# LN2's variance and bias on ScalarE, squares from the raw sum, and a new order of all queues: an adaLN block with sliding-window attention and a gated FFN

## Chip, cores and metric

One NeuronCore of one Trainium2 chip runs the whole program. The metric is the device time of one execution in microseconds; the time before is the median of three runs. All times on the trace count from the start of the profiled span.

## What is computed

```python
mod = (silu(c) @ w_mod).reshape(1, 6, 1, -1)        # sa, ca, ga, sb, cb, gb
h = layernorm(x) * (1 + ca) + sa
x = x + ga * A(h, wqkv, wo)      # 32 heads of 16; each position looks at 8 earlier ones, 2 apart
h = layernorm(x) * (1 + cb) + sb
x = x + gb * ((silu(h @ w1) * (h @ w3)) @ w2)
```

x has 2048 positions of 512 columns, the FFN is 1792 wide, all bf16. A layernorm takes mean and variance over the 512 columns. The first is called LN1 here, the second LN2.

## The kernel before

The 2048 positions are 16 tiles T of 128. Each stage is a set of ops that Python code records, and each op has one engine and a key. In the texts an op is called by its key, as here:

- LN1 (ln_stats, lines 549 to 580): statistics on VectorE and GpSimd, normalization on VectorE. Then q, k and v products on TensorE (lines 691, 711), evacuated by ScalarE (700, 701, 721). v goes to DRAM.
- Attention per tile: `pq` (line 742) is VectorE's product of q with eight shifted copies of k, 128x4096. `lg` on TensorE (752) sums it by head into logits. `sm` are five VectorE ops of the softmax (764, 769, 794 to 797) around `ex`, the exponential on ScalarE (782); it works on two tiles at a time. `at` turns the weights on TensorE (807), evacuated by ScalarE (811). `vl` are four loads of shifted v by SP. `av` is VectorE's product of v and weights (827), 128x4096. `ac` on TensorE (855) sums it, evacuated by ScalarE (861). `ot` is a transposing DMA. `wo` is the output product (867). `rs` is VectorE's residual sum (871), which also gives the row's sum `sx`.
- LN2 (ln_sums, lines 582 to 604), by pairs of tiles (0,1), (2,3) and so on: `nm = -sx/512` on GpSimd (586); squares of `x + nm` with their sum on ScalarE (590), for each tile; variance plus epsilon (596), the power -0.5 (597) and the bias `nm * rs` (599) on GpSimd; normalization `x*rs + nb` on ScalarE (601), for each tile. ln_T then transposes, by TensorE (636, evacuated at 644) for the groups 0 and 1, by DMA (`tr`) for the groups 2 to 5, which ScalarE then scales and shifts in place (621).
- FFN in six groups of tiles: (0,1), (2,3), (4..7), (8..11), (12,13), (14,15). `Fg.f` is column block f (of 14) of group g. It has two halves on TensorE (883), four matmuls each, of 256 columns where the group has two tiles and 512 where it has four: the gate, which ScalarE takes through Silu (889), and the up half, which VectorE multiplies with it (892). `zT.0` and `zT.1` are the two halves of tile T's output product (921; 909 for the last two tiles, which are cut by columns), each over seven blocks. `zo` adds x on VectorE (931), and SP stores. `mod7` to `mod10` scale w2's rows by gb on VectorE (952).

Silu and the exponential need different tables on ScalarE; a load of 1.28 us stands at each of the nine switches. `lg` and `ac` use a quarter of TensorE's columns at a time (tiled products).

Every result has a buffer from a pool: eight PSUM banks, 20 buffers of FFN products, five of normalized rows, three of shifted v, and so on. An op that writes a buffer waits for all users of the value that held it before. All engines take their instructions in order.

The order isn't found by a scheduler at run time. `ORDER` lists all ops by number, `SLOTS` a buffer for every pooled value, and `Program.place` cuts `ORDER` into one queue for each engine and for SP. `Program.synchronize` puts in the waits that the recorded dependences need, including waits of an engine for an own earlier result. Each op carries a planned `cost` in ns for whoever works such a list out, and a `lock` flag that marks the long VectorE products and GpSimd's ops. ScalarE's small new ops have a planned cost of 80, the power 600.

Of the kernel before, what the change touches and what calls it, by code (L numbers as in the profile page):

```python
# [10 lines left out]
P = 128  # L11
# [245 lines left out]
def c_act(n):  # L257
    return 66 + n * 107 // 128
# [14 lines left out]
def _build(p, A_x, A_wqkv, A_wo, B_w1, B_w3, B_w2, c, w_mod, out):  # L273
# [308 lines left out]
    def ln_sums(Ts):  # L582

        n, i, k = len(Ts), Ts[0], ("st", NT + Ts[-1])
        vnm, vvs, vns = Val("nmean"), [], [Val("xn", xnpool) for T in Ts]
        p.op("pool", lambda e: e.tensor_scalar(nm[:, i:i + n, 0], sx[:, i:i + n, 0], -1.0 / D, None, op0=ALU.mult), 215, k,  # L586
             r=[vsx[T] for T in Ts], w=[vnm])
        for T, vn in zip(Ts, vns):
            vv = Val("var")
            p.op("act", lambda e, vn=vn, T=T: e.activation(vn.at[:], x_sb[:, T, :], ACT.Square, bias=nm[:, T, :],  # L590
                                                    accum_out=var[:, T, :]), c_act(512) + 212, ("st", NT + T), r=[vx[T], vnm],
                 w=[vv, vn])
            vvs.append(vv)
        va, vr, vb = Val("vare"), Val("rstd"), Val("nbias")
        rsn = rs[:, NT + i:NT + i + n, 0]
        o = p.op("pool", lambda e: e.tensor_scalar(rsn, var[:, i:i + n, 0], 1.0 / D, EPS, op0=ALU.mult, op1=ALU.add), 210, k, r=vvs, w=[va])
        o = p.op("pool", lambda e: e.tensor_tensor(rsn, rsn, bass.AP(cst, 1, [[2, P], [0, n]]), ALU.pow), 600, k, r=[va, vcst],
                 w=[vr], lead=o)
        p.op("pool", lambda e: e.tensor_tensor(nb[:, i:i + n, 0], nm[:, i:i + n, 0], rsn, ALU.mult), 210, k, r=[vr, vnm], w=[vb], lead=o)  # L599
        for T, vn in zip(Ts, vns):  # L600
            p.op("act", lambda e, vn=vn, T=T: e.activation(vn.at[:], x_sb[:, T, :], ACT.Identity, bias=nb[:, T, :],  # L601
                                                           scale=rs[:, NT + T, :]),
                 c_act(512) + 212, ("nm", NT + T), r=[vx[T], vr, vb], w=[vn])
        return vns
# [472 lines left out]
```

## Time and profile before

| what | value |
|---|---|
| median of 3 runs | 238.1 us (237.95 to 238.78) |
| profiled execution, own time | 239.43 us |
| its span on the trace | 237.7 us |
| granted TensorE clock | 1.00 throughout |
| squares, line 590 | 16 of 0.71 us, and 16 reads of the accumulator of 0.19 |
| variance 596, power 597, bias 599 on GpSimd | 8 each, median 0.19, 0.70 and 0.20 us |
| normalization, line 601 | 16 of 0.81 us |
| products of VectorE, lines 742 and 827 | 16 each, 2.28 and 2.29 us |

A line of the profile's groups gives the source line, engine, operation, output and inputs by the program's names, shapes and count, then busy time and the mean ns of one, then the idle time ahead of it and what ended it. A line of the waits gives engine and line, what it waited for, and microseconds in all, times and the longest. A line of the timeline gives start and length in microseconds. A busy TensorE is one that has a matmul under way; matmuls overlap, so a wait shorter than one's fill shows only in the distance of their starts: 0.109 us for 256 columns and 0.216 for 512 when nothing is in the way.

### The profile page before, as it was taken

The page shows a single profiled execution, that of the slowest core. Times are in us where ns is not written, and L with a number is a line of the kernel's source. Part 1 is how long each engine was busy: PE and PEld are TensorE (multiplying, and loading weights), DVE is VectorE, ACT ScalarE, POOL GpSimd, SP SyncE. Part 2 cuts the span into 40 slices and gives each one's busy share as a digit, 9 for nine tenths or more (in the row PEclk, how much of TensorE's full clock was granted, in tenths as well). Part 3 has the DMA queues.
Part 4 walks back from the last instruction along what each step waited for, and adds up shares of the span by engine and source line. Part 5 has one row for each costly group of instructions (what it writes and reads, how often), then busy time and mean ns, then how long its engine had stood idle before and what let it go on. Part 6 is the DMA issues. An engine that isn't in the chain of part 4 may idle for free.

```text
span 237.7 us, 4535 instructions
## 1 busy us (share of the span) xinstructions
PE 229.7 (97%) x1781; PEld 136.2 (57%) x1806; DVE 179.4 (75%) x279; ACT 138.5 (58%) x267; POOL 29.2 (12%) x66
## 2 busy tenths in 40 slices
PE   7999999999999998999999999999999999999995
PEld 4776454445588674664444444444475457485774
DVE  5699999999999989999999999682654403434433
ACT  2289577999978744985865594837473405040300
POOL 4434100013002000240002520012010000000000
PEclk9999999999999999999999999999999999999999
DMA  6999999999999999897981693642203000000202
GB/s 216 372 337 322 158 237 299 208 269 283 353 200 270 243 249 199 173 260 177 247 234 47 182 234 72 154 132 46 67 19 91 3 0 0 6 19 0 70 0 88
DMA packets 46317, 38.85 MB, mean 163 GB/s; under 512 B 21704, under 2 KB 37080, under 8 KB 46296
## 3 DMA queue, kind: packets, MB, share of 16 engines
q1 hardware_dynamic: 46288, 38.56, 66.9%
q8 instruction: 14, 0.23, 0.4%
q14 instruction: 7, 0.06, 0.1%
q10 hardware_dynamic: 8, 0.00, 0.0%
HBM read 29.62 MB, written 4.21 MB: 142 GB/s over the span
## 4 chain that ended last, share of the span: by engine, by line
PE 74%; DMA 8%; DVE 8%; SPq 4%; ACT 3%; issue 2%; ACTq 0%; DVEq 0%
PE pall L883 38%; PE pall L921 18%; DMA sb_x<-in_A_x_dram 5%; PE pall L867 5%; SPq L124 4%; PE pall L691 4%; DMA sb_vsh<-v_scratch_dram 3%; PE pall L909 3%; PE pall L855 2%; PE pall L752 2%; PE pall L711 2%; DVE sb_vsh L827 2%; DVE sb_pq L742 2%; DVE sb_hh L892 1%; ACT sb_h L621 1%
## 5 line engine op out<-in xcount | busy, mean ns | idle before, releaser
L883 PE MATMUL pall<-sb_h,sb_w 128*128 128x256 bf16 (+1 forms) x664 | 101.9, 307 | 1.8 <-DVE sb_hh L892 0.9
L883 PEld LDWEIGHTS pall<-sb_h,sb_w 128*128 128x128 bf16 x672 | 64.8, 98 | 37.2 <-issue 2.8
L889 ACT ACTIVATE sb_sg<-pall 128x256 bf16<-128x256 f32 (+1 forms) x84 | 35.6, 453 | 54.1 <-PE pall L883 53.0
L892 DVE TENSOR_TENSOR sb_hh<-sb_sg,pall 128x256 bf16<-128x256 bf16 (+1 forms) x84 | 39.9, 505 | 34.8 <-PE pall L883 32.7
L921 PE MATMUL pall<-sb_w,sb_hh 128*128 128x512 bf16 x190 | 44.0, 379 | 0.3
L742 DVE TENSOR_TENSOR sb_pq<-sb_q,sb_kT 128x4096 bf16<-128x4096 bf16 x16 | 36.3, 2282 | 0.0
L921 PEld LDWEIGHTS pall<-sb_w,sb_hh 128*128 128x128 bf16 x196 | 19.0, 98 | 21.6 <-DVE sb_hh L892 0.4
L691 PE MATMUL pall<-sb_h,sb_wqkv 128*128 128x512 bf16 (+1 forms) x154 | 30.2, 335 | 0.5 <-issue 0.2
L827 DVE TENSOR_TENSOR sb_vsh<-sb_vsh,sb_al 128x4096 bf16<-128x4096 bf16 x12 | 27.3, 2287 | 2.1 <-DMA sb_vsh<-v_scratch_dram 2.1
L621 ACT ACTIVATE sb_h<-sb_h,sb_modc 128x512 bf16<-128x512 bf16 (+1 forms) x24 | 16.5, 743 | 10.1 <-DMA sb_h<-sb_xn 10.1
L691 PEld LDWEIGHTS pall<-sb_h,sb_wqkv 128*128 128x128 bf16 x160 | 14.7, 98 | 11.8 <-ACT sb_ac L861 0.4
L931 DVE TENSOR_TENSOR sb_o<-pall,sb_x 128x512 bf16<-128x512 f32 (+1 forms) x18 | 11.1, 625 | 10.5 <-PE pall L921 6.8
L711 PE MATMUL pall<-sb_wqkv,sb_h 128*128 128x512 bf16 x62 | 15.5, 379 | 0.2
L867 PE MATMUL pall<-sb_wo,sb_ot 128*128 128x512 bf16 x61 | 15.3, 379 | 0.3 <-issue 0.2
L586 POOL TENSOR_SCALAR sb_nm<-sb_sx 128x2 f32<-128x2 f32 x8 | 1.7, 218 | 105.2 <-DVE sb_x L871 105.1
L644 ACT ACTIVATE sb_h<-pall,sb_modc 128x256 bf16<-128x256 bf16 (+1 forms) x18 | 9.9, 612 | 7.5 <-DVE sb_modc L509 6.5
L861 ACT ACTIVATE sb_ac<-pall 128x512 bf16<-128x512 f32 x16 | 9.5, 595 | 7.2 <-PE pall L855 7.1
L601 ACT ACTIVATE sb_xn<-sb_x,sb_nb,sb_rs 128x512 bf16<-128x512 bf16 x16 | 12.4, 806 | 0.7 <-POOL sb_nb L599 0.6
L871 DVE SCALAR_TENSOR_TENSOR sb_x<-pall,sb_x 128x512 bf16<-128x512 f32 x16 | 10.9, 686 | 1.5 <-PE pall L867 1.3
L590 ACT ACTIVATE sb_xn<-sb_x,sb_nm 128x512 bf16<-128x512 bf16 x16 | 11.4, 714 | 0.7 <-POOL sb_nm L586 0.7
L721 ACT ACTIVATE sb_v<-pall 128x512 bf16<-128x512 f32 x16 | 9.5, 600 | 2.8 <-PE pall L711 2.8
L555 DVE BATCH_NORM_STATS2 sb_st<-sb_x 128x6 f32<-128x512 bf16 x16 | 10.6, 680 | 0.8 <-DMA sb_x<-in_A_x_dram 0.7
(87 smaller groups left out, 208.3 us busy)
## 6 DMA issues: line engine op xcount, KB each, us to landing
sb_vsh<-v_scratch_dram SPq DMA_DIRECT2D x48, 256.0 KB, 5.5
sb_vshx<-v_scratch_dram SPq DMA_DIRECT2D x16, 256.0 KB, 4.6
sb_w<-in_B_w_dram SPq DMA_DIRECT2D x6, 512.0 KB, 7.9
sb_w<-in_B_w_dram SPq DMA_DIRECT2D x6, 384.0 KB, 5.4
v_scratch_dram<-sb_v SPq DMA_DIRECT2D x16, 128.0 KB, 6.4
out_dram<-sb_o SPq DMA_DIRECT2D x14, 128.0 KB, 1.8
sb_wqkv<-in_A_wqkv_dram SPq DMA_DIRECT2D x6, 256.0 KB, 6.3
sb_x<-in_A_x_dram SPq DMA_DIRECT2D x4, 256.0 KB, 6.4
```

What stands on the lines that cost most here:

```text
L590: p.op("act", lambda e, vn=vn, T=T: e.activation(vn.at[:], x_sb[:, T, :], ACT.Square, bias=nm[:, T, :], accum_out=var[:, T, :]), c_act(512 ...
L601: p.op("act", lambda e, vn=vn, T=T: e.activation(vn.at[:], x_sb[:, T, :], ACT.Identity, bias=nb[:, T, :], scale=rs[:, NT + T, :]), c_act(5 ...
L621: return e.activation(vh.at[:, ft, 0:n * P], vh.at[:, ft, 0:n * P], ACT.Identity, bias=modc[:, 8 * which + ft:8 * which + ft + 1], scale=m ...
L691: ins = e.matmul(bank(vp)[:, j * n:(j + 1) * n], wqkv[:, t, col:col + P], vh.at[:, t, 0:n], start=(t == ORDER[0] and j == 0), stop=(t == O ...
L711: ins = e.matmul(bank(vp), vh.at[:, t, tt * P:(tt + 1) * P], wqkv[:, t, 2 * D:3 * D], start=(t == ORDER[0]), stop=(t == ORDER[-1]))
L742: return e.tensor_tensor(vp.at[:], in0, in1, ALU.mult)
L827: return e.tensor_tensor(v_w, v_w, a_w, ALU.mult)
L867: ins = e.matmul(bank(vy), vt.at[:, ft, :], wo[:, ft, :], start=(ft == 0), stop=(ft == KT - 1))
L883: ins = e.matmul(bank(vp)[:, 0:n], wt[:, t, fi * P:(fi + 1) * P], vh.at[:, t, 0:n], start=(t == 0), stop=(t == KT - 1))
L889: p.op("act", lambda e: e.activation(vt.at[:, 0:n], bank(vgp)[:, 0:n], ACT.Silu), c_act(n), k, r=[vgp], w=[vt], table="silu")
L892: p.op("dve", lambda e: e.tensor_tensor(vh_.at[:, 0:n], vt.at[:, 0:n], bank(vup)[:, 0:n], ALU.mult), c_dve(n), k, r=[vt, vup], w=[vh_])
L921: ins = e.matmul(bank(vz), vhh[fi].at[:, tt * P:(tt + 1) * P], w2[:, fi, :], start=(fi == 0), stop=(fi == NF - 1))
```

## The change

```diff
-            p.op("act", lambda e, vn=vn, T=T: e.activation(vn.at[:], x_sb[:, T, :], ACT.Square, bias=nm[:, T, :],
-                                                    accum_out=var[:, T, :]), c_act(512) + 212, ("st", NT + T), r=[vx[T], vnm],
+            p.op("act", lambda e, vn=vn, T=T: e.activation(vn.at[:], x_sb[:, T, :], ACT.Square, bias=sx[:, T, :], scale=-float(D),
+                                                    accum_out=var[:, T, :]), c_act(512) + 212, ("st", NT + T), r=[vx[T], vsx[T]],
...
-        o = p.op("pool", lambda e: e.tensor_scalar(rsn, var[:, i:i + n, 0], 1.0 / D, EPS, op0=ALU.mult, op1=ALU.add), 210, k, r=vvs, w=[va])
-        o = p.op("pool", lambda e: e.tensor_tensor(rsn, rsn, bass.AP(cst, 1, [[2, P], [0, n]]), ALU.pow), 600, k, r=[va, vcst],
-                 w=[vr], lead=o)
-        p.op("pool", lambda e: e.tensor_tensor(nb[:, i:i + n, 0], nm[:, i:i + n, 0], rsn, ALU.mult), 210, k, r=[vr, vnm], w=[vb], lead=o)
+        p.op("act", lambda e: e.activation(rsn, var[:, i:i + n, 0], ACT.Identity, bias=cst[:, 0:1], scale=float(D) ** -3), 80, ("va", NT + Ts[-1]),
+             r=vvs + [vcst], w=[va])
+        p.op("pool", lambda e: e.tensor_tensor(rsn, rsn, bass.AP(cst, 1, [[2, P], [0, n]]), ALU.pow), 600, k, r=[va, vcst], w=[vr])
         for T, vn in zip(Ts, vns):
+            vb = Val("nbias")
+            o = p.op("act", lambda e, T=T: e.activation(nb[:, T, :], nm[:, T, :], ACT.Identity, bias=0.0, scale=rs[:, NT + T, :]), 80,
+                     ("nb", NT + T), r=[vr, vnm], w=[vb])
             p.op("act", lambda e, vn=vn, T=T: e.activation(vn.at[:], x_sb[:, T, :], ACT.Identity, bias=nb[:, T, :],
                                                            scale=rs[:, NT + T, :]),
```

The squares are of `-512*x + sx`, which is -512 times the old argument, so they need the row's sum but not the mean; the variance instruction scales by 512^-3. In the changed kernel squares stay at line 590, the variance is ScalarE's at 596 (one for a pair), the power stays GpSimd's at 598, the bias is ScalarE's at 601 (one for each tile) and the normalization is at 603. GpSimd's mean stays at 586 and is needed by the bias alone. ScalarE gets 24 instructions more, GpSimd 16 fewer; all others are the same in kind and number.

`ORDER` and `SLOTS` are new (not shown). Decoded, the queues are the same up to the FFN's first group, about 77 us into the span, but for the new instructions and some bank numbers. Behind it all queues differ. ScalarE's around LN2, where V is the variance, B a bias, n a normalization, sq a square, and F a Silu:

| tiles | before | after |
|---|---|---|
| 0,1 | sq0 sq1 k k q q q at2 n1 n0 k v | sq0 sq1 k k q q V q at2 B1 n1 B0 n0 k v |
| 2,3 | sq2 sq3 F0.8 at6 n3 n2 v F0.10 | sq2 sq3 F0.8 V B2 B3 n3 n2 F0.10 at6 |
| 4 to 7 | sq4 sq5 F1.4 sq6 sq7 F1.5 F1.10 n5 n4 F1.13 at8 n6 n7 | sq5 sq4 V B4 n4 sq7 sq6 V B5 n5 B6 n6 B7 n7 F1.13 at8 |
| 8,9 | sq8 ac11 sq9 ac10 F F F F F n8 F ... n9 | sq8 sq9 V F ac10 B8 n8 ac11 F F F B9 n9 |
| 10,11 | ex12 sq10 sq11 F n10 at12 n9 n11 | sq11 ex12 sq10 V B11 B10 n10 n11 at12 |
| 12,13 | sq13 sq12 F ac14 F F ac15 n12 F F n13 | sq12 sq13 V B13 n13 B12 F F n12 F F F ac15 ac14 |
| 14,15 | sq15 sq14 F F F F n15 F n14 | sq15 sq14 V F F F B14 n14 F F F F B15 n15 |

TensorE's between the transposes of group 1 and the first block of group 2 (xN is a number of halves):

```
before  z0.0 F1 x6 lg8 ac4 F1 x9 ac7 F1 wo5 ac6 F1 wo4 F1 wo7 z0.1 wo6 F1 x5 z1.1 F1 x3 at8 F1 x2 z2.0 z3.0 z3.1 z2.1 ac9 lg11 lg10 ac8
after   z0.0 F1 x8 lg8 ac4 F1 x12 ac7 wo5 F1 ac6 wo4 F1 x5 wo7 wo6 z1.1 z0.1 at8 F1 x2 z2.0 z3.0 z2.1 z3.1 ac9 lg11 lg10 ac8
```

VectorE's there: before, `av4 F1.11 F1.2 sm av7`, then three blocks and `av6`; after, `av4 F1.1 F1.2 F1.5 sm av7 F1.3 sm`, four blocks and `av6`; F1.13 stands behind `pq11` and `pq10` in both. SP issues the loads of v for the tiles 4 and 7 ahead of tile 12's store of v instead of behind it, two loads of w2 between later loads of v, and for the tiles 12 and 13 the transposes of LN2 (`tr18`) ahead of ot15 and ot14 instead of behind them.

More of the change, by code (lines that the diff above doesn't have):

```diff
@@ L589, in ln_sums @@
             vv = Val("var")
-            p.op("act", lambda e, vn=vn, T=T: e.activation(vn.at[:], x_sb[:, T, :], ACT.Square, bias=nm[:, T, :],
-                                                    accum_out=var[:, T, :]), c_act(512) + 212, ("st", NT + T), r=[vx[T], vnm],
+            p.op("act", lambda e, vn=vn, T=T: e.activation(vn.at[:], x_sb[:, T, :], ACT.Square, bias=sx[:, T, :], scale=-float(D),
+                                                    accum_out=var[:, T, :]), c_act(512) + 212, ("st", NT + T), r=[vx[T], vsx[T]],
                  w=[vv, vn])
             vvs.append(vv)
-        va, vr, vb = Val("vare"), Val("rstd"), Val("nbias")
+        va, vr = Val("vare"), Val("rstd")
         rsn = rs[:, NT + i:NT + i + n, 0]
-        o = p.op("pool", lambda e: e.tensor_scalar(rsn, var[:, i:i + n, 0], 1.0 / D, EPS, op0=ALU.mult, op1=ALU.add), 210, k, r=vvs, w=[va])
-        o = p.op("pool", lambda e: e.tensor_tensor(rsn, rsn, bass.AP(cst, 1, [[2, P], [0, n]]), ALU.pow), 600, k, r=[va, vcst],
-                 w=[vr], lead=o)
-        p.op("pool", lambda e: e.tensor_tensor(nb[:, i:i + n, 0], nm[:, i:i + n, 0], rsn, ALU.mult), 210, k, r=[vr, vnm], w=[vb], lead=o)
+        p.op("act", lambda e: e.activation(rsn, var[:, i:i + n, 0], ACT.Identity, bias=cst[:, 0:1], scale=float(D) ** -3), 80, ("va", NT + Ts[-1]),
+             r=vvs + [vcst], w=[va])
+        p.op("pool", lambda e: e.tensor_tensor(rsn, rsn, bass.AP(cst, 1, [[2, P], [0, n]]), ALU.pow), 600, k, r=[va, vcst], w=[vr])
         for T, vn in zip(Ts, vns):
+            vb = Val("nbias")
+            o = p.op("act", lambda e, T=T: e.activation(nb[:, T, :], nm[:, T, :], ACT.Identity, bias=0.0, scale=rs[:, NT + T, :]), 80,
+                     ("nb", NT + T), r=[vr, vnm], w=[vb])
             p.op("act", lambda e, vn=vn, T=T: e.activation(vn.at[:], x_sb[:, T, :], ACT.Identity, bias=nb[:, T, :],
```

127 rows, old and new, of tables (ORDER, SLOTS) are left out of this document.

## The prediction

> **What bounds the kernel.** First the busy times, then a table by stretches.
>
> ```profile
> PE 229.7 (97%) x1781; PEld 136.2 (57%) x1806; DVE 179.4 (75%) x279; ACT 138.5 (58%) x267; POOL 29.2 (12%) x66
> ```
> ```profile
> 0.00:8.00 8.00, 6.24 (x64) 4.42 (x65) 4.87 (x19) 1.59 (x2) 4.42 (x20) 1.00 0.78 259
> 8.00:88.00 80.00, 78.89 (x745) 49.40 (x753) 75.88 (x115) 64.38 (x125) 10.62 (x22) 1.00 1.14 269
> 88.00:96.00 8.00, 6.72 (x55) 3.74 (x55) 8.00 (x12) 3.81 (x7) 0.00 (x0) 1.00 0.94 194
> 96.00:232.00 136.00, 134.84 (x901) 76.14 (x914) 88.81 (x132) 68.72 (x134) 14.14 (x24) 1.00 0.40 97
> 232.00:237.70 5.70, 3.02 (x28) 2.46 (x26) 1.87 (x4) 0.00 (x0) 0.00 (x0) 1.00 0.26 82
> ```
> The columns behind the length are TensorE, weight load, VectorE, ScalarE, GpSimd. TensorE idles 8.0 us: 1.8 at the start and 2.7 at the end, which the change doesn't touch, 1.3 in 88 to 96, and 2.3 in pieces over 216 us, mostly at the entries and exits of the tiled products. Those runs number 14 before and after, so at most about 2 us can be won. VectorE is full (75.9 of 80, then 8.0 of 8) while attention lasts. Next the waits:
>
> ```profile
> ACT sb_xn L590 <- POOL sb_nm L586: 0.7, 2, 0.3
> ACT sb_xn L601 <- POOL sb_nb L599: 0.6, 1, 0.6
> PE pall L883 <- DVE sb_hh L892: 0.9, 1, 0.9
> PE pall L855 <- DVE sb_vsh L827: 0.4, 1, 0.4
> ```
> ScalarE waits for GpSimd 1.3 us in the whole run, and TensorE never for LN2 beyond 0.2 us: LN2's chain is long but covered. The two waits of TensorE are the hole of 88 to 96. Starts of matmuls show it wider than idle time does: 1.14 us between two starts at 88.68 where 0.11 is the rule, and 0.53 too much at 92.44, together **1.56 us**. Last, the chain itself, GpSimd and then VectorE around the first pair:
>
> ```profile
> 52.75 0.19 POOL L596 TENSOR_SCALAR sb_rs<-sb_var 128x2 f32<-128x2 f32 x1 [1.64 <-ACT sb_xn L590]
> 53.03 0.71 POOL L597 TENSOR_TENSOR sb_rs<-sb_rs,sb_cst 128x2 f32<-128x2 f32 x1
> 53.81 1.82 POOL L599 TENSOR_TENSOR sb_nb<-sb_nm,sb_rs 128x2 f32<-128x2 f32 x1
> ```
> ```profile
> 53.31 2.28 DVE L742 TENSOR_TENSOR sb_pq<-sb_q,sb_kT 128x4096 bf16<-128x4096 bf16 x1
> 55.58 2.28 DVE L742 TENSOR_TENSOR sb_pq<-sb_q,sb_kT 128x4096 bf16<-128x4096 bf16 x1
> ```
> L599 takes 0.20 when undisturbed; here it started inside VectorE's product and ended 0.05 behind it. All five GpSimd instructions of LN2 that started inside a product (at 53.81, 101.65, 129.03, 131.99, 159.52) took 1.5 to 2.1 us and ended with it; the power of 53.03, started before one, kept its 0.71.
>
> **The change, part by part.** ScalarE's durations come from these rows:
>
> ```profile
> L889 ACT ACTIVATE sb_sg<-pall 128x256 bf16<-128x256 f32 x56 | 20.1, 382 | 35.9 <-PE pall L883 35.5
> L889 ACT ACTIVATE sb_sg<-pall 128x512 bf16<-128x512 f32 x28 | 15.8, 597 | 18.2 <-PE pall L883 17.6 <-DVE sb_hh L892 0.5
> L590 ACT ACTIVATE sb_xn<-sb_x,sb_nm 128x512 bf16<-128x512 bf16 x16 | 11.4, 714 | 0.7 <-POOL sb_nm L586 0.7
> L601 ACT ACTIVATE sb_xn<-sb_x,sb_nb,sb_rs 128x512 bf16<-128x512 bf16 x16 | 12.4, 806 | 0.7 <-POOL sb_nb L599 0.6
> ```
> 256 columns more cost 0.215, so 512 cost 0.43; what is left is 0.17 without a per-partition operand (L889), 0.28 with one (L590), 0.37 with two (L601). The small instructions have one: **0.28 us**, bounds 0.17 and 0.80 (L601 whole). Neighbours on ScalarE overlap by 0.1 (evacuations of 0.6 start 0.475 apart); behind an own result that is lost, so a bias and its normalization take about 0.4 more than the normalization alone. 24 instructions at 0.28 are 6.7 us on an engine that idles 99: no bound as a sum, only by place.
>
> GpSimd loses sixteen 0.20 us instructions and keeps the power. Unblocked, the chain isn't shorter: before, from the squares' end (75.54, second pair) to the bias (76.97), 1.43; after, the read of the accumulator 0.1, variance 0.28, power 0.70, bias 0.28, hops 0.15, that is 1.5. Gained are 0.3 at its head (no wait for the mean) and fewer chances of a block. Lost is the cover: the variance wakes GpSimd, and in four of eight pairs the bias stands right behind it, so ScalarE stops for the power and all that queues behind stops too (evacuations, Silu, and through them TensorE's banks).
>
> *Stage 1, 50 to 64 us; order as before but for the new instructions.* The squares start 0.40 earlier (50.75 for 51.15: the exponential ahead ends, no mean is waited for). The variance stands behind four evacuations: 51.87 + 0.72 - 0.40 + 4 x 0.475 gives 54.09 to 54.37. The product of 53.31 runs to 55.59, so the power is let in at 55.6 and ends at about 56.15 (0.05 plus the 0.5 by which it exceeds a small one; bounds 0.05 and 0.70 behind the product). First bias 56.2, first normalization 56.53 (before 55.67), second 57.58 (before 56.40), all behind it 1.2 late. ScalarE has no gap from there to 61.5, where TensorE's first FFN matmuls follow the last evacuation by 0.05. They start 1.2 late; 0.3 returns where TensorE waited for VectorE at 63.94: **+0.9**. VectorE takes the delay over by 68 (its fourth FFN product follows TensorE by 0.05).
>
> *Stage 2, 64 to 100.* VectorE gets it back at 87.14, where it stood 1.04 for a load of v that doesn't move; TensorE now has 20 half units of FFN group 1 ahead of ac7 instead of 15. Summed at 0.436 a half from 82.8, I find no instruction whose bank isn't free; the nearest (F1.0, waiting for F1.3 on VectorE at 90.2) is due at 91.2. Both holes close: **-1.55** (bounds -1.55 and 0, if another product of VectorE comes late in their place), so about -0.7 in all at wo6 (99.1, same work before 99.85).
>
> *Stage 3, 100 to 113.* In ScalarE's queue: squares 7 and 6, variance, bias and normalization 5, bias and normalization 6, then 7, then F1.13's Silu, then at8. Squares end 102.25, variance 102.75. VectorE's product started at 102.1 and runs to 104.4; power until 105.0; biases and normalizations 6 and 7 until 107.2; Silu 107.55; product on VectorE 108.0. Tile 2's second half needs it and was due at 107.05: **+1.05**. The transposes follow the last normalization (107.2; before 106.18); from the last issue to h took 2.4 us before, so h is ready at 112.9 and TensorE asks at 113.2: covered by 0.3.
>
> *Stage 4, 113 to 180.* From sums of work ahead: at14 waits 0.2 for VectorE, at12 0.1. For tiles 12 and 13 the power meets av14 (161.8 to 164.05 here); F3.2's Silu stands behind two biases and a normalization until 166.5, then F3.6 until 168.25 where F3.9 wants its bank at 168.0. With wo15's transpose now queued behind two others on SP: **+0.8** (bounds 0 and 2.3, one blocked product). Behind 180 TensorE has only FFN work; the last four output pieces end as before: 0.
>
> SP's other moves (loads of v ahead of v12's store, w2 between them) shift issues by 0.5 to 1.2 us and land under VectorE's queue: 0, at most 1.0, the wait of 87.14.
>
> Sum: 0.9 - 1.55 + 1.05 + 0.8 = **+1.2 us**. The profiled execution took 239.43 around a span of 237.7 and would take 240.6; that execution stands 1.33 over the median of 238.1, so the forecast is **239.3**.
>
> **Rivals.** *The power is let in* (not slower). If it starts ahead of the product, or a product doesn't hold it, stage 1 costs 0.25 and stage 3 0.2, with a stall of 0.2 back in stage 2: 0.25 - 1.35 + 0.2 = -0.9, **237.2**. For it: all eight powers before took 0.69 to 0.71. Against: none of those started inside a product, they followed a small instruction that had waited in their place; in stage 1 the variance ends 1.1 us behind the product's start, and 0.65 behind it in stage 3; it decides once those margins are gone.
>
> *Small instructions are dear.* If each costs 0.25 more (queue drained, two operands), stage 1 grows by 0.75, stage 3 by 0.5 (two biases behind the power), stage 4 by 0.5: +2.95, **241.1**. For it: every second one waits on its own engine. Against: the rows of 0.28 and 0.37.
>
> *The power holds the product back.* Let in at 55.6 it would keep the next product waiting 0.55, again at 104.45; VectorE is full until 150, so +1.1: **240.4**. Against: the product at 53.31 started during a power, yet L742 takes 2277 to 2286 ns in all 16. The Trainium skill (SBUF — State Buffer, Who interferes with whom) says that whichever of the two starts first has the shared ports for its whole instruction and the other fully blocks; by that this rival would hold. The trace agrees for GpSimd (1.5 to 2.1 us) and not for VectorE.
>
> **Chances.** What this measurement can tell from no change is about 0.5%, 1.2 us. Forecast 0.46 (own range 238.4 to 240.3, split 0.25 within, 0.21 slower); power let in 0.24 (0.12 faster, 0.12 within); dear 0.22 (0.03 within, 0.19 slower); held back 0.08 slower. Faster 0.12, within 0.40, slower 0.48. The range runs from 237.0 to 241.4, leaving a part of the first rival below and of the second above.
>
> **What would show it.** L598 at 1.5 us or more for the pairs of 54 and 103 us; ScalarE idle in front of L601 for GpSimd, 3 us or more in all (before 0.6); TensorE idle near 58 and 107, and under 0.3 in 88 to 96; L596 and L601 near 0.28. If TensorE waits instead behind 113 by over 2 us, or the powers are all 0.70, the working is wrong.

## The result, and the profile after

The changed kernel takes 241.5 us (median of 241.19, 241.53 and 241.97) beside 238.4 for the kernel before on the same chip: **ratio 1.0131, 95% interval 1.0094 to 1.0169**. It is slower, by more than forecast (239.3) and just above the range's upper end (241.4). A fourth run of 246.3 us, with a granted clock of 0.993, is left out. A second measurement, among the experiments, gave 1.0086 (1.0056 to 1.0116).

The profiled execution took 241.97 us around a span of 240.1, so 2.5 us more than that of before (239.43, 237.7). Lines behind 595 have moved down by two (L742 is now L744, L827 L829, L867 L869, L883 L885, L892 L894); L598 is the power. The busy times of the page:

```profile
PE 232.2 (97%) x1806; PEld 135.9 (57%) x1806; DVE 179.6 (75%) x279; ACT 145.0 (60%) x291; POOL 22.6 (9%) x50
```
The 2.5 us that TensorE's busy time grew by are no work: both kernels run the same 1806 matmuls, and the trace of before lacks the records of 25 of them. ScalarE has its 24 instructions more (6.5 us; 6.7 were reckoned), GpSimd 6.6 us less. The stretches, columns as before:

```profile
88.00:96.00 8.00, 8.00 (x73) 5.47 (x71) 8.00 (x10) 6.93 (x14) 0.00 (x0) 1.00 1.16 238
96.00:104.00 8.00, 6.86 (x42) 3.77 (x40) 6.51 (x18) 5.44 (x16) 1.44 (x4) 1.00 1.12 227
104.00:120.00 16.00, 14.87 (x114) 7.10 (x113) 14.90 (x12) 10.27 (x17) 2.58 (x1) 1.00 0.62 139
120.00:232.00 112.00, 112.00 (x730) 62.01 (x729) 67.72 (x104) 56.00 (x117) 5.14 (x8) 1.00 0.32 80
```
The hole of 88 to 96 is gone, as forecast. TensorE now idles 1.1 us in 96 to 104 and 1.1 in 104 to 120, where before had 0.05 and 0.2; behind 120 it never stops. The waits name both places:

```profile
ACT sb_nb L601 <- POOL sb_rs L598: 6.0, 6, 1.8
...
PE pall L869 <- DMA sb_ot<-sb_ac: 1.1, 2, 0.6
...
PE pall L885 <- ACT sb_h L623: 0.5, 1, 0.5
```
ScalarE's biases wait 6.0 us for the power (3 or more were forecast). L869 is the output product `wo`, which waits for attention's transposing DMA: no step of the prediction has that. L885 is the FFN, waiting for h at the entry of group 2. The groups give the prices:

```profile
L598 POOL TENSOR_TENSOR sb_rs<-sb_rs,sb_cst 128x2 f32<-128x2 f32 x8 | 10.1, 1266 | 17.4 <-ACT sb_rs L596 17.4
...
L601 ACT ACTIVATE sb_nb<-sb_nm,sb_rs 128x1 f32<-128x1 f32 x16 | 4.4, 288 | 6.0 <-POOL sb_rs L598 6.0
...
L596 ACT ACTIVATE sb_rs<-sb_var,sb_cst 128x2 f32<-128x2 f32 x8 | 2.4, 299 | 0.2
```
The small ScalarE instructions cost 0.29 and 0.30 us (0.28 reckoned). The power's mean of 1.27 hides two kinds, 0.7 to 0.8 and 1.6 to 2.8. GpSimd's timeline, then VectorE's products beside it:

```profile
54.67 1.59 POOL L598 TENSOR_TENSOR sb_rs<-sb_rs,sb_cst 128x2 f32<-128x2 f32 x1 [3.45 <-ACT sb_rs L596]
...
103.82 2.76 POOL L598 TENSOR_TENSOR sb_rs<-sb_rs,sb_cst 128x2 f32<-128x2 f32 x1 [0.95 <-ACT sb_rs L596]
```
```profile
53.41 2.28 DVE L744 TENSOR_TENSOR sb_pq<-sb_q,sb_kT 128x4096 bf16<-128x4096 bf16 x1
...
103.73 2.28 DVE L744 TENSOR_TENSOR sb_pq<-sb_q,sb_kT 128x4096 bf16<-128x4096 bf16 x1
```
The power asked for at 54.67 ends at 56.26, 0.57 behind the product of 53.41. That of 103.82 came 0.09 behind the start of pq11, which ended at 106.02 with pq10 close behind; it ended 0.56 behind pq11, inside pq10. pq10 was not held up: the two products together take 4.49, beside 4.48 in product_later, where no power was caught between them.

**Where the time went.** For each op of TensorE, the start in the changed trace is set against the moment at which the trace of before had started the same amount of TensorE's work. Here and in all that follows an op's start is that of its first weight load, of which no record is missing; where nothing waits, the first matmul starts 0.1 to 0.2 us later. The difference is the lateness, and its growth between fixed ops a step. The ops are wo1 (49 us), the seventh half unit of F0 (65), ac7 (92), wo6 (99), the first of FFN group 2 (113) and the fourth of group 4 (180).

| run | to 49 | 49 to 65 | 65 to 92 | 92 to wo6 | wo6 to group 2 | to 180 |
|---|---|---|---|---|---|---|
| *prediction* | 0 | +0.9 | -1.55 | 0 | +1.05 | +0.8 |
| changed kernel | -0.10 | +0.98 | -1.53 | **+1.61** | **+1.46** | +0.05 |
| same, after_again | +0.56 | +0.97 | -1.57 | +0.31 | +1.50 | -0.12 |
| same, after_c | +2.56 | +0.97 | -1.58 | +1.27 | +1.47 | -0.13 |
| *before*, before_d | -0.13 | -0.09 | **-1.00** | -0.31 | +0.20 | +0.12 |
| order_alone | +0.08 | -0.09 | -1.58 | +1.13 | **+3.34** | +1.62 |
| code_alone | +0.49 | +0.97 | -0.66 | -0.40 | **+3.84** | +1.69 |
| code_early | +0.44 | +0.19 | -0.34 | -0.20 | +0.35 | +0.58 |
| var_early | +0.18 | **+0.17** | -1.57 | +0.90 | +1.47 | -0.09 |
| loads_behind | +0.03 | +0.97 | -1.58 | **-0.09** | +1.74 | +0.12 |
| product_later | +3.62 | +0.98 | -1.58 | +1.22 | **+0.37** | -0.07 |
| all_three | +0.17 | +0.18 | -1.58 | -0.09 | +1.79 | -0.02 |
| all_four | +0.30 | +0.13 | -1.58 | -0.09 | +2.01 | -0.13 |
| pieces | +1.04 | +0.17 | -1.58 | -0.09 | **+0.54** | +0.04 |
| old_chain_gap | +2.45 | -0.08 | -1.59 | -0.09 | +3.12 | +1.52 |

What stands under "to 49" differs between executions of one kernel. The steps behind it repeat to 0.2, but for that of wo6. How the amount of work is counted matters too: by starts of matmuls, with lg and ac at the 0.44 us that separates their starts from the next op's, single steps come out up to 0.4 different (the step to wo6 1.8 for 1.61, in loads_behind 0.3 for -0.09). The sizes below are good to about that much.

### The profile page after: what moved, and what is told of

Same layout as the page of the kernel before. It is cut to its first block, busy times and chain, and to the rows that moved or that the text cites. A ratio compares the mean times of both kernels' runs of the same rounds, so it can differ in the third digit from the quotient of the medians.

```text
span 240.1 us, 4567 instructions
## 1 busy us (share of the span) xinstructions
PE 232.2 (97%) x1806; PEld 135.9 (57%) x1806; DVE 179.6 (75%) x279; ACT 145.0 (60%) x291; POOL 22.6 (9%) x50
## 4 chain that ended last, share of the span: by engine, by line
PE 83%; ACT 8%; DMA 4%; DVE 2%; POOL 2%; issue 1%; ACTq 0%
PE pall L885 40%; PE pall L923 14%; PE pall L693 9%; PE pall L869 5%; PE pall L713 4%; PE pall L857 3%; PE pall L754 3%; PE pall L911 3%; ACT sb_h L623 2%; DMA sb_h<-sb_xn 2%; POOL sb_rs L598 2%; DMA sb_ot<-sb_ac 2%; PE pall L638 1%; ACT sb_xn L603 1%; ACT sb_xn L590 1%; DVE sb_st L555 1%
## 5 line engine op out<-in xcount | busy, mean ns | idle before, releaser
L885 PE MATMUL pall<-sb_h,sb_w 128*128 128x256 bf16 (+1 forms) x672 | 102.2, 308 | 0.5 <-ACT sb_h L623 0.5
L885 PEld LDWEIGHTS pall<-sb_h,sb_w 128*128 128x128 bf16 x672 | 65.1, 98 | 36.1 <-issue 1.7
L894 DVE TENSOR_TENSOR sb_hh<-sb_sg,pall 128x256 bf16<-128x256 bf16 (+1 forms) x84 | 39.7, 505 | 28.6 <-PE pall L885 23.7
L891 ACT ACTIVATE sb_sg<-pall 128x256 bf16<-128x256 f32 (+1 forms) x84 | 35.0, 454 | 42.9 <-PE pall L885 42.1
L923 PE MATMUL pall<-sb_w,sb_hh 128*128 128x512 bf16 x196 | 45.1, 379 | 0.6 <-DVE sb_hh L894 0.6
L744 DVE TENSOR_TENSOR sb_pq<-sb_q,sb_kT 128x4096 bf16<-128x4096 bf16 x16 | 36.2, 2282 | 0.0
L693 PE MATMUL pall<-sb_h,sb_wqkv 128*128 128x512 bf16 (+1 forms) x160 | 31.0, 337 | 0.4 <-DVE sb_st L555 0.3
L829 DVE TENSOR_TENSOR sb_vsh<-sb_vsh,sb_al 128x4096 bf16<-128x4096 bf16 x12 | 27.3, 2287 | 3.8 <-DMA sb_vsh<-v_scratch_dram 3.7
L869 PE MATMUL pall<-sb_wo,sb_ot 128*128 128x512 bf16 x64 | 16.0, 379 | 1.1 <-DMA sb_ot<-sb_ac 1.1
L713 PE MATMUL pall<-sb_wqkv,sb_h 128*128 128x512 bf16 x64 | 16.0, 379 | 0.0
L590 ACT ACTIVATE sb_xn<-sb_x,sb_sx 128x512 bf16<-128x512 bf16 x16 | 11.5, 722 | 7.0 <-DVE sb_x L873 6.9
L598 POOL TENSOR_TENSOR sb_rs<-sb_rs,sb_cst 128x2 f32<-128x2 f32 x8 | 10.1, 1266 | 17.4 <-ACT sb_rs L596 17.4
```

The lines of the kernel that those rows point to most:

```text
L693: ins = e.matmul(bank(vp)[:, j * n:(j + 1) * n], wqkv[:, t, col:col + P], vh.at[:, t, 0:n], start=(t == ORDER[0] and j == 0), stop=(t == O ...
L713: ins = e.matmul(bank(vp), vh.at[:, t, tt * P:(tt + 1) * P], wqkv[:, t, 2 * D:3 * D], start=(t == ORDER[0]), stop=(t == ORDER[-1]))
L744: return e.tensor_tensor(vp.at[:], in0, in1, ALU.mult)
L829: return e.tensor_tensor(v_w, v_w, a_w, ALU.mult)
L869: ins = e.matmul(bank(vy), vt.at[:, ft, :], wo[:, ft, :], start=(ft == 0), stop=(ft == KT - 1))
L885: ins = e.matmul(bank(vp)[:, 0:n], wt[:, t, fi * P:(fi + 1) * P], vh.at[:, t, 0:n], start=(t == 0), stop=(t == KT - 1))
```

## The experiments

**Order and code apart.** Two kernels, each with one half of the change.

```diff
 order_alone: ORDER and SLOTS of the changed kernel
-ScalarE: sq sq V ... B n B n ...          GpSimd: power
+ScalarE: sq sq ... n n ...                GpSimd: mean (ahead of the squares), variance, power, bias
 code_alone: ORDER and SLOTS of before
-ScalarE: sq sq ... n n ...                GpSimd: mean, variance, power, bias
+ScalarE: sq sq ... V ... B n B n ...      GpSimd: mean, power   (V where GpSimd's variance stood)
```

> The changed kernel's order with the old LN2 chain (variance, power and bias by pairs on GpSimd, squares that wait for the mean). My theory: the loss has two sources of about equal size, the order (ot7 and ot6 land later because loads of v for tile 8 are issued ahead of and between them, TensorE +1.75 us between 92 and 101) and ScalarE's stops for a blocked power (stage 1 +0.9, stage 3 about +1). Then the order alone gives -1.6 (both holes of 88 to 96 closed) +1.75 and a little for GpSimd blocked near 104, in all +0.5 us on before: ratio 1.002, between 0.998 and 1.008; no lateness of TensorE at 65 us, and wo6 1.0 us or more behind. Rival, all of the loss is in the code: ratio 0.993 or less. Rival, all of the loss is in the order: ratio 1.011 or more.

> The order of before with the new LN2 chain put into it (variance on ScalarE where GpSimd's stood, each bias right ahead of its normalization). My theory: stage 1 late by 0.9 us at 65, swallowed by VectorE's wait of 1.04 for the load of v at 87; behind 100 a bias that stops ScalarE for a power that meets a VectorE product, +1 to +2 us: ratio 1.006, between 1.002 and 1.010. Rival, all of the loss is in the code: 1.011 or more. Rival, all of it is in the order: 0.998 to 1.002.

Measured: ratio 1.0239 (1.0194 to 1.0284) and 1.0272 (1.0228 to 1.0317). Each half alone costs about twice what both together cost, so both expectations fall. Both are above the 1.011 of the rival that blames that half alone, but these two can't both be true, and the sum of the halves is not the whole. order_alone has no lateness at 65, as expected, and loses 3.34 between wo6 and group 2. GpSimd's timeline there:

```profile
103.07 1.57 POOL L596 TENSOR_SCALAR sb_rs<-sb_var 128x2 f32<-128x2 f32 x1 [1.64 <-ACT sb_xn L590]
104.73 2.63 POOL L597 TENSOR_TENSOR sb_rs<-sb_rs,sb_cst 128x2 f32<-128x2 f32 x1
107.44 0.19 POOL L599 TENSOR_TENSOR sb_nb<-sb_nm,sb_rs 128x2 f32<-128x2 f32 x1
```
```profile
102.31 4.48 DVE L742 TENSOR_TENSOR sb_pq<-sb_q,sb_kT 128x4096 bf16<-128x4096 bf16 x2
```
The second fence is VectorE's, pq11 and pq10 in one line. The old chain meets both products in turn: the variance waits for pq11 to end, the power, asked for inside pq10, for pq10. In the order of before, five short FFN products of VectorE stood between the two, and the power went through there (asked at 103.25, 0.69). In code_alone the variance of tiles 6 and 7 stood behind F1.13 and at8, its power met pq10 (2.70 us), and group 2 waited for h. A line of its waits:

```profile
PE pall L885 <- ACT sb_h L623: 3.6, 1, 3.6
```
TensorE's wait in its timeline, and two stretches, where the third column from the end is the granted clock:

```profile
117.08 5.10 PE L885 MATMUL pall<-sb_h,sb_w 128*128 128x512 bf16 x15 [3.56 <-ACT sb_h L623]
116.00:120.00 4.00, 2.92 (x7) 1.02 (x8) 1.44 (x2) 3.95 (x7) 0.00 (x0) 0.64 0.90 266
120.00:124.00 4.00, 4.00 (x19) 1.81 (x18) 3.93 (x4) 2.26 (x3) 0.00 (x0) 0.93 1.25 255
```
No matmul was under way for 3.56 us, until 117.08, and then the clock was 0.64 and 0.93. Part of the step "to 180" is this.

**The code alone, better placed.**

```diff
 code_alone, ScalarE, tiles 0,1:      -sq0 sq1 k k q q V q at2
                                      +sq0 sq1 V k k q q q at2
 code_alone, ScalarE, tiles 6,7:      -sq6 sq7 F1.5 F1.10 B5 n5 B4 n4 F1.13 at8 V
                                      +sq6 sq7 V F1.5 F1.10 B5 n5 B4 n4 F1.13 at8
 and so for the pairs 2,3 and 8,9; in the other four V stood there already
```

> The order of before with the new chain, each variance right behind the second of its squares (in the run code_alone two of the eight stood further back, that of tiles 6 and 7 behind F1.13 and at8, where its power met pq10 and took 2.70 us). My theory: the power of 6 and 7 is asked near 102.4, inside pq11, is let in when that ends at 103.7, among VectorE's short FFN products, and is done by 104.5; the second FFN group then starts near 113.3 (before 112.84, code_alone 117.07): ratio 1.004, between 1.000 and 1.009 (code_alone 1.027). Rival, the new chain costs ScalarE too much wherever the variance stands: 1.015 or more.

Ratio 1.0054 (1.0033 to 1.0075), group 2 at 113.28: as expected. The power of 6 and 7 was asked for at 102.17 inside pq11 and ended at 103.97, among the short FFN products. So the code by itself costs about half a per cent, and the rest of code_alone's 2.7 was the place of variances. Four were moved; the steps name two, that of tiles 0 and 1 (to 65: 0.19 for 0.97) and that of 6 and 7 (behind wo6: 0.35 for 3.84).

**The first stop.**

```diff
 ScalarE
-sq0 sq1 k k q q V q at2 B1 n1 B0 n0
+sq0 sq1 V k k q q q at2 B1 n1 B0 n0
```

> The changed kernel with one change: ScalarE's variance of tiles 0 and 1 right behind the two squares, ahead of the four evacuations it followed. My theory (the first power is 1.59 us because it was asked for 1.1 us behind the start of VectorE's product): the power now starts near 52.5, ahead of that product, takes 0.70, ScalarE doesn't stop for it, and TensorE is late by 0.0 to 0.3 us at 65 instead of 0.89; most of it lasts to the end: ratio to before 1.010. Rival, the lateness at 65 comes from the three small instructions themselves and not from the stop: 0.6 or more remains at 65. Rival, the 0.9 is taken back later in any case (a load of v at 87, av6 at 94.7): late by 0.2 at 65 but 1.013 at the end.

GpSimd's timeline:

```profile
53.04 0.70 POOL L598 TENSOR_TENSOR sb_rs<-sb_rs,sb_cst 128x2 f32<-128x2 f32 x1 [1.54 <-ACT sb_rs L596]
```
The power now runs ahead of the product (53.69) and takes 0.70. The step to 65 falls from 0.98 to 0.17, and the later steps don't take that back: the small instructions cost 0.2, the stop 0.8. Ratio 1.0068 (1.0033 to 1.0103), with the 1.010 expected still inside the interval.

**The output product's wait.** `ot7` and `ot6` are the transposes of attention's result that wo7 and wo6 need. In the order of before SP issues the loads of v for tile 8 behind both; in the changed order two of them stand ahead of ot7 and a third between the two. The description of the change above doesn't name this move. The run puts the three behind ot6, and the store of v15 one place back.

```diff
 SP
-ot4 vl8 vl8 load24 ot7 vl8 ot6 vl9 vl9 v15 vl9 vl9 tr14 vl8 tr14
+ot4 load24 ot7 ot6 vl9 vl9 vl8 vl9 vl9 vl8 vl8 tr14 v15 vl8 tr14
```

> The changed kernel with one change: on SP the three loads of shifted v for tile 8 that stand ahead of and between ot7 and ot6 are issued behind ot6. My theory (the transposing DMAs land late because of them: 4.9 and 4.0 us from issue to the product that needs them, before at most 3.3 and 3.4): ot6 is issued near 96.2 instead of 96.8, wo7 starts at about 98.4 (99.13 in the changed kernel), wo6 at 99.5 (100.78), and about 1 us of it reaches the end: ratio to before 1.009 (the changed kernel 1.013). Rival, the transposes land late whatever stands beside them, or the FFN's second group waits for ScalarE anyway: wo6 within 0.3 of 100.8 or the end unchanged, 1.013.

What the trace answers for the tile `ot` between 90 and 103 us, from issue to landing, first in the changed kernel, then in this one:

```profile
DMA to landing us min/median/max: 4.0/4.4/4.8
```
```profile
DMA to landing us min/median/max: 2.3/2.3/2.3
```
wo7 started at 98.39 and wo6 at 99.15 without a wait, and the step to wo6 is gone. The steps behind 49 add up to 1.16 us at 180 instead of 2.57; the interval of the timed ratio, 1.0113 (1.0059 to 1.0167), is too wide to show it alone. Four more traces have the loads behind ot6 (all_three, all_four, pieces, old_chain_gap), and in all of them the step is gone. The Trainium skill (DMA: Bandwidth & Descriptors, Queues, rings and completion order) says that SP has one ring on each of the 16 DMA engines, and that each engine consumes its ring in order. By that a transpose waits for the loads of 256 KB that were issued ahead of it, and the trace agrees: 2.3 us without them, 4.0 to 4.8 behind them.

**A margin of 0.1 us.**

```diff
 VectorE
-sm8 rs7 rs6 sm8 F1.8 F1.9 pq11 pq10
+rs7 rs6 sm8 sm8 F1.8 F1.9 pq11 pq10
```

> The changed kernel with one change: on VectorE one softmax operation of the tiles 8 and 9 (0.55 us) moves from ahead of rs7 to behind rs6, so the product pq11 starts about 0.5 us later. In the changed kernel the variance of tiles 6 and 7 ended at 103.73 and pq11 started at 103.73; the power asked at 103.82 and took 2.76. My theory: a margin of 0.1 us decides 2 us; the power now takes 0.70, the biases of tiles 6 and 7 start near 104.7 instead of 106.6, the hole ahead of z2.1 shrinks from 1.09 to about 0.8, and TensorE's second FFN group starts near 114.1 instead of 115.26: ratio to before 1.008 (changed kernel 1.013). Rival, the power is slow there for another reason: 1.5 us or more, and no gain.

GpSimd's timeline:

```profile
107.09 0.70 POOL L598 TENSOR_TENSOR sb_rs<-sb_rs,sb_cst 128x2 f32<-128x2 f32 x1 [0.95 <-ACT sb_rs L596]
```
This execution was 3.6 us late from its first 40 us on; pq11 started at 107.60, the power half a microsecond ahead of it. The step between wo6 and group 2 falls from 1.46 to 0.37. Ratio 1.006 (1.0027 to 1.0093). In these traces one softmax operation of 0.55 us, moved by two places on VectorE, which has no other part in this wait, is worth 1.1 us. The margin is not always that small. The power came 0.08 to 0.09 behind pq11's start in three traces (the changed kernel, after_c, var_early), but 0.34 behind it in after_again and 0.55 in loads_behind, where wo7 and wo6 were earlier. That a move of 0.55 is enough there too, no run with this change alone shows.

**All of it together.**

```diff
 all_three = loads_behind + var_early + product_later, and on ScalarE
-V5 B4 n4 sq7 sq6 V7 B5 n5 B6 n6 B7 n7 F1.13 at8
+V5 sq7 sq6 V7 B4 n4 B5 n5 F1.13 B6 n6 B7 n7 at8
 all_four = all_three, and
-SP: v15 tr14 vl8 tr14          VectorE: pq11 pq10 F1.13
+SP: v15 vl8 tr14 tr14          VectorE: pq11 F1.13 pq10
```

> The changed kernel with the loads of v behind ot6, the first variance right behind its squares, the softmax operation behind rs6, and on ScalarE the squares and the variance of tiles 6 and 7 ahead of the biases of 4 and 5, with F1.13's Silu ahead of the biases of 6 and 7. My theory: these were three separate losses and they add up: wo6 near 99.0 (100.78), the power of tiles 6 and 7 asked near 102.0, ahead of pq11, 0.70 us; no hole of 1 us ahead of z2.1; the second FFN group at about 112.6 (115.26; before 112.84), so no later than before: ratio 0.999, between 0.994 and 1.004. Rival, the group is held by the transposing DMAs and the four scalings behind them whatever LN2's chain does: 113.5 or later, ratio 1.005 or more.

> The run all_three with two moves more: on SP the last load of v for tile 8 is issued ahead of LN2's four transposes for the tiles 4 to 7 instead of between them, and on VectorE F1.13's product stands between pq11 and pq10 instead of behind both. In all_three the four transposes were issued back to back from 102.71 to 108.78 and the second FFN group waited for h until 113.31. My theory: the group is now bound by SP's issues of the transposes and the four scalings of 0.8 behind them; the last transpose leaves 0.6 earlier, the group starts near 112.65, the hole of 0.73 ahead of z2.1 closes without a gain of its own: 0.6 us less than all_three, ratio to before 1.005, between 1.001 and 1.009. Rival, the group is bound by VectorE's av8 and ac8 (TensorE is through with ac8 at 111.7): the same 113.3.

Ratios 1.0073 (1.0042 to 1.0103) and 1.0061 (1.0021 to 1.0100). wo6 (98.50) and the power (101.73, 0.70) came as expected, group 2 did not: 113.31 and 113.61 for 112.6 and 112.65. The three losses don't add up, because with the first two out of the way the group waits for h by another path. For all_four I had named SP's issues as that path. The last transpose was issued earlier (106.79 for 107.24), yet the first scaling began later (110.62 for 110.32): the transposes now took 4.9 us to land (median) for 4.1, behind one load of v more. In 108 to 110 the DMA engines (share and GB/s at the end of the line) show it; all_three, then all_four:

```profile
108.00:110.00 2.00, 1.95 (x10) 0.87 (x9) 2.00 (x2) 0.00 (x0) 0.00 (x0) 1.00 0.66 132
```
```profile
108.00:110.00 2.00, 1.95 (x13) 0.78 (x15) 2.00 (x2) 0.00 (x0) 0.00 (x0) 1.00 1.50 158
```
The rival falls too: ac8 started at 111.59, and TensorE waited behind it for the scaled h:

```profile
PE pall L885 <- ACT sb_h L623: 1.6, 1, 1.6
```
What bounds the entry is the landing of the transposes and the four scalings of 0.8 behind it, 2.93 us in a row on ScalarE.

```diff
 pieces = all_four, VectorE's zo0 right behind av8, each scaling of group 2 as a value of its own (not shown), and in ffn_unit
...
+        if gi == 2 and fi in (2, 3):
+            for j, t in enumerate(SCALED):
+                def part_mm(e, t=t, j=j):
+                    return e.matmul(bank(vgp)[:, 0:n], w1[:, t, fi * P:(fi + 1) * P], vh.at[:, t, 0:n], start=(j == 0),
+                                    stop=(j == KT - 1))
+                o = p.op("pe", part_mm, c_mm(n), k, r=[vh.pieces[t], vw1[g]], part=[vgp], hold=[vh],
+                         after=after)
...
```

> The run all_four with the gates of F2.2 and F2.3 cut into four matmuls that each wait for one of the four scalings of h, interleaved, and zo0 right behind av8 on VectorE so that F2.3's bank is free. My theory: TensorE resumes near 111.8, behind ac8, instead of 112.65, and 1.0 to 1.3 us less is idle in 112 to 114: ratio to before 1.000, between 0.996 and 1.005. Rival, TensorE is held later by the next thing (ScalarE's evacuations and Silus behind the scalings): no gain on all_four.

Ratio 0.9991 (0.9959 to 1.0023). The step falls from 2.01 to 0.54, and the ratio by 0.7% against all_four: the new code in the new order, mended in all these places, stands where before stood. No version here beats it. The cut into pieces is a change that before doesn't have, and what it would be worth there was not run.

**The old chain with a gap.**

```diff
 order_alone + loads_behind + product_later, all_four's vl8, F1.13's Silu ahead of n6 and n7, and on VectorE
-F1.8 F1.9 pq11 pq10 F1.13
+pq11 F1.8 F1.9 F1.13 pq10
```

> The changed kernel's order with the old LN2 chain on GpSimd (order_alone, ratio 1.024), with the loads of v behind ot6, the softmax operation behind rs6, and F1.8, F1.9 and F1.13 between pq11 and pq10 on VectorE as a gap for GpSimd. My theory: the old chain loses in this order where three GpSimd instructions in a row meet products that stand back to back (1.57, 2.63 there); with a gap of 1.0 us the variance and the power are done in it, the bias perhaps blocked once; stage 1 has no stop. TensorE 1.7 us ahead at 92, 1.5 ahead at wo6, the second FFN group near 112.5 to 113.5; the pair of 12 and 13 still meets av14 (+1.4 in order_alone): ratio 1.008, between 1.000 and 1.014. Rival, the old chain can't be fed in this order at all: 1.02 or more.

Ratio 1.0129 (1.0081 to 1.0177), group 2 later than expected. In the gap the power alone went through (0.70, asked at 106.01); the variance had waited 1.50 for pq11, and the bias, asked at 106.79, was caught by pq10 and took 2.34. Three instructions in a row don't fit into a gap of 1.0 us.

**The same kernels again.** The forecast had taken off 1.33 us, by which the traced execution of before stood above its median.

> The kernel before once more, nothing changed: a second trace of it. Its undisturbed runs lie between 237.7 and 240.9 us, and the first profiled execution (239.43) is 1 us above most. My theory: the spread comes from the first 50 us, where w_mod and the other weights arrive (in the traces of the experiments TensorE's third product of the modulation starts between 0.0 and 2.5 us later than in the first trace of before, and what is lost there stays): with a time of T, TensorE is late by T - 239.4 within 0.5 at 49 us already, and no step of more than 0.3 follows. Rival, the spread comes from waits spread over the run: no difference at 49 us beyond 0.3 where the times differ by 0.8 or more.

> The changed kernel once more, nothing changed, beside before on the same chip: ratio 1.011 to 1.015 if the first measurement (1.0131, from 1.0094 to 1.0169) holds; in the trace TensorE late against the first trace of before by 0.9 at 65, ahead by 0.8 at 92, late by 1.0 at wo6, by 2.4 at the second FFN group, each within 0.2 once the difference of the first 49 us is taken off. Rival, one of these steps belonged to one execution only: it is missing here.

> The kernel before, nothing changed, for a trace of one of its shorter executions (238.4 or less; both traces so far are of 239.3 and 239.4, and agree within 0.4 us at every point). Theory A: the shorter ones are early from the start (weights land earlier), so TensorE is ahead by 1 us at 49 already. Theory B: they are the same up to 85 and save the two holes of 88 to 96 or the wait for h at 113, waits that depend on when a DMA lands: ahead only behind 88. If the time is 239 or more, a third trace like the first two, and nothing is told apart.

> As before_c: the kernel before, nothing changed. If it takes 238.4 or less, theory A has TensorE ahead of the first trace by 1 us at 49 us, theory B ahead only behind 88; at 239 or more it tells nothing new.

> As before_c: the kernel before, nothing changed. If it takes 238.4 or less, theory A has TensorE ahead of the first trace by 1 us at 49 us, theory B ahead only behind 88; at 239 or more it tells nothing new.

> The changed kernel, nothing changed, a third trace. Of its two traces one lost 1.75 us at wo7 and wo6 (the transposing DMAs landed 4.0 to 4.9 us behind their issue), the other 0.3 (2.3 to 3.3). Theory: how long the transposes take depends on whether the loads ahead of them are through when they are issued, and this varies from run to run: the step here lies between 0.2 and 1.8, and goes with the landing time. All other steps as in both traces within 0.3: +1.0 by 65, -1.7 between 65 and 92, +1.5 between wo6 and the second FFN group, 0 behind it.

before_again took 239.29 and equals the first trace within 0.4 at every point. before_c (240.49) and before_e (240.36) lost 1.8 and 2.5 us ahead of 51 and 30 us: the longer executions do lose in the first 50 us, as the expectation of before_again had it, and say nothing of the shorter ones. before_d took 238.21, and is one. VectorE at av7, first in the first trace of before, then in before_d, and before_d's stretch:

```profile
87.14 2.29 DVE L827 TENSOR_TENSOR sb_vsh<-sb_vsh,sb_al 128x4096 bf16<-128x4096 bf16 x1 [1.04 <-DMA sb_vsh<-v_scratch_dram]
85.92 2.29 DVE L827 TENSOR_TENSOR sb_vsh<-sb_vsh,sb_al 128x4096 bf16<-128x4096 bf16 x1
88.00:96.00 8.00, 7.66 (x59) 4.13 (x59) 8.00 (x15) 5.08 (x8) 0.22 (x1) 1.00 0.62 156
```
No wait, and TensorE idles 0.34 us in 88 to 96 for 1.28: theory B. Of the 1.2 us that this execution saves, 1.0 lie in the hole that the change closes. before_c and before_e say the same from the other side: their lateness of 1.8 and 2.5 was 0.6 and 1.1 behind the hole, which took up the rest. Why the load landed in time (its issue was 0.6 earlier) is open.

after_again: ratio 1.0086 (1.0056 to 1.0116), with the lower end of the expected 1.011 to 1.015 just inside the interval. All steps came back within 0.2 but that of wo6, 0.31 for 1.61. Its ot7 and ot6 landed in 2.3 and 3.3 us, those of after_c (step 1.27, 244.16 us) in 4.2 and 3.4, those of the first trace in 4.0 and 4.8: that step goes with the landing time and varies from execution to execution, as expected of after_c.

## Why the forecast was wrong

- *Stage 1, +0.9*: right in three traces (0.97 to 0.98), and for its reason: without the blocked power 0.17 is left.
- *Stage 2, -1.55*: right against the traced execution (-1.53 to -1.58). **The step that failed is the one behind the sum, "that execution stands 1.33 over the median ... so the forecast is 239.3".** The prediction counted the hole of 88 to 96 as a gain and then took off the 1.33 by which the traced execution was long. before_d, the one short execution that was traced, shows that these are largely the same microseconds: 1.0 of the 1.2 that it saves lie in that hole. Against such an execution stage 2 gives -0.55 (-1.55 + 1.00), and the prediction's own terms come to 238.1 + 0.9 - 0.55 + 1.05 + 0.8 = 240.3.
- *SP's moves, 0, at most 1.0*: **the second step that failed**. They cost 0.3 to 1.6 at wo6. The prediction looked at the loads of v, which did land under VectorE's queue, and not at the transposes that follow them in the same queue; the three loads of tile 8 ahead of ot6 it doesn't name.
- *Stage 3, +1.05*: mis-sized, 1.46 to 1.50. Its chain was right: the power asked for behind pq11's start, its end 0.56 behind pq11's end, 0.94 of lateness at z2.1. Of the 0.65 by which it put the variance's end behind pq11's start, 0.09 were left in the first trace and 0.55 in loads_behind. "Covered by 0.3" was not: from the last transpose's issue to the first scaling took 3.27 us (109.01 to 112.28) instead of 2.44, so h was late by another 0.5.
- *Stage 4, +0.8*: mis-sized, nothing (-0.13 to +0.05), which by luck made up for part of the terms above. The power of tiles 12 and 13 was asked for at 164.77 and took 0.71, since av14 started only at 166.14, behind 2.63 us of waiting for its load of v; at 130.68 a power of 2.16 cost TensorE nothing.
- *The rivals*: "small instructions are dear" falls (0.29 and 0.30 us; 0.2 for three in stage 1), though its 241.1 was nearest. "The power let in" falls for the two pairs that mattered. "The power holds the product back" falls: the 16 products of L744 have a mean of 2.28, pq10 among them.

With measured sizes: 238.1 + 0.97 - 0.55 + 1.5 + 0 and 0.3 to 1.6 for wo6 gives 240.3 to 241.6; measured were 241.2 to 242.0 in the first measurement and 240.9 to 242.2 in the second. That before itself had medians of 239.3 to 239.8 on other chips, while the changed kernel's stayed at 241.4 to 241.5, is not explained by the one cause that a trace shows. TensorE's idle time of 8.0 us in the prediction contains what the 25 missing records leave open (an estimate that fills each in at a usual length makes it 6.7); no term rests on it.

## What to carry to other kernels

Before the gap between a traced execution and the median is subtracted, ask which wait made that execution long; if the change removes that wait, the gap is already spent. A short instruction that shares its engine's access with long ones is priced by where its request falls, here 0.1 us deciding 2 in one trace, so its distance to the next long one belongs into the order as a margin. A transposing DMA on the path should be the next thing in its queue: here loads sent ahead of it that nobody needed yet cost 0.3 to 1.6 us.

## What the runs showed of the hardware

- A GpSimd instruction caught by VectorE's two-input product of 2.28 us gets through at the boundary to the next one even if VectorE leaves no gap: the power of 103.82 ended 0.56 us behind the boundary, inside pq10, and the two products together took 4.49 us, beside 4.48 where none was caught (product_later). VectorE's short FFN products, which read one input from PSUM, hold nothing up: a power among five of them took 0.69 (before, 103.25), and one that had waited for pq11 was through 0.57 behind its end (code_early, 103.97).
- After 3.56 us without a matmul TensorE's granted clock was 0.64 and then 0.93 over two stretches of 4 us (code_alone). After 1.63 us (all_four, until 113.84) it stayed at 1.00. The Trainium skill (TensorE: Matmul & The Clock Gate, HAM oscillation — how this bites in real kernels) puts the limit for idle gaps at about 3.4 us; both cases agree.
- A transposing DMA of 128 by 512 took 2.3 us from issue to landing in the five traces whose loads of tile 8 stand behind ot6 (loads_behind, all_three, all_four, pieces, old_chain_gap), 2.3 to 4.8 with the loads ahead (the three traces of the changed kernel), and 8.2 right behind four loads (ot5 at 83 us, before).
